# A dilated convolution with shared differences: signs moved into the differences, the first loads in halves, the last outputs on three queues

## The chip, the cores and the metric

The kernel runs on one core of a Trainium2 chip. The metric is device time in microseconds (us), the median of several runs. One further execution is taken with the hardware profiler; its page and its trace are what is read below. Engines are named as on the page: PE is TensorE, PEld its weight load, DVE VectorE, ACT ScalarE, POOL GpSimd, SP SyncE; SPq and ACTq are the DMA issues of SP and ACT.

## The reference

Fifteen taps, two time steps apart, of a causal convolution from 144 to 288 channels, then a gate and a projection:

```python
B, T, D, K = (2, 16000, 144, 15)        # x [B,T,D], w [K,D,2D], w_o [D,D], all bfloat16
xp = jnp.pad(x, ((0, 0), (28, 0), (0, 0)))
h = sum over i of einsum('btc,cd->btd', xp[:, 28 - 2*i : 28 - 2*i + T, :], w[i])
z = jnp.tanh(h[..., :D]) * sigmoid(h[..., D:])
return z @ w_o
```

## The kernel before

**Tiling.** Each of the two sequences is cut into 8 windows of 2000 outputs (16 windows in all), loaded as 2048 + 32 time steps. A window has two octets (`rho` 0 and 1), 32 octets in all; an octet is eight output rows of 128 positions each, 16 time steps apart. The 144 input channels are split into 128 and a remainder of 16.

**Input.** `load` (L82 to L90) brings the 128 channels of a window in by one transposing DMA: the tile `xn`, channels on partitions. The remainder takes two steps. `gather` (L92 to L100) copies the 16 channels, in packets of 32 bytes, from DRAM to a DRAM scratch `xg`, sorted by the time step modulo 4 (`r=4` blocks). `remainder` (L102 to L105) then reads `xg` back by a transposing DMA so that eight taps of 16 channels lie on the 128 partitions: the tile `rx`.

**Sharing by differences.** The convolution of eight output rows isn't done tap by tap. Sums of weights are multiplied with the signal, and other weights with differences of the signal in time, and results are shared between rows, so that an octet takes 72 matmuls of 128x128 by 128x288 where each row by itself would take more. `derive_steps` (L111 to L141) makes the differences on VectorE: d2, d4, d8 from `xn`, d48 from d4, d28 and d24 from d2, and `re` (L129 to L137, two instructions) from `rx`. Where a difference is needed with the other sign, the weights are negated: `a1e`, `an`, `bcn` on VectorE (`neg`, L194), `wn` on ACT (L210), made once at the start from `w_all`, together with the sums `sm`, `ss`, `a1v`, `av`, `bc`, `bcv`, `s_r`, `ns_r` (L197 to L224).

**An octet** has three leaves in the PSUM pool `a` (A1, A2, A3) and two in the pool `bc` (B1, C1). A leaf computes what two rows share (`common`), ACT copies the bank (`copy`), then each row adds its own part (`private`). `direct` (L297) adds the taps on d24 and `re` for the rows B2, B3, C2 and C3, into banks that ACT copied (`dup`). VectorE combines (`q`, `out_y`) in FP32; ACT does tanh and sigmoid; VectorE multiplies to `z`. A transposing DMA on SP turns `z` to `zt` (`z_load`, L330), 12 matmuls project it (`outproj`, L351), ACT copies to the output tile `o` (`project_out`, L359), and `store` (L364) writes a window of 125 rows of 4608 bytes, issued on SP.

**Order.** The order is written by hand: `PLAN` (L16 to L23) lists the steps of one octet with an offset in octets, and `todo` (L441) sorts all octets' steps by octet plus offset, then by place in the list. Each engine and queue works in that order. `xg:-6` places a gather six octets ahead of the octet that uses it, `xl:-3` a load, `rx0:-2` the read of the scratch. `late` (L226) puts `re` and `d24` of the first window where they are first needed. SP's queue thus carries, for each window: a gather, a load, an rx, two zt and a store. Buffers: two of `xn` and `rx`, two of `o`, two PSUM banks for `a`, five for `bc`, one for `po`.

**Start.** The remainder's weights come by 15 small DMAs, seven from POOL (`wo_p`) and eight from ACT (`we_r`), L181 to L184. The first load, `w_all` in four parts (L178, L179) and the first rx are on SP, the first gather on ACT. TensorE does 20 warm-up matmuls on zeros.

**End.** The last octet's `z` is transposed by TensorE (`z_by_pe`, L335). Five stores remain after the last convolution matmul, all on SP: window 14 whole, one half of window 15 (rows of 288 bytes), and the other half in three pieces (L431 to L434).

Of the kernel before, what the change touches and what calls it, by code (L numbers as in the profile page):

```python
# [9 lines left out]
F32 = mybir.dt.float32  # L10
# [6 lines left out]
    po0:3 yB2_0:0 m0a:1 g1:3 q3_0:0 ost:4 pA3_1:0 sg1:1 kC:0 B2_1:0 q3_1:0 po1:3 vA1:-1 g2:3 pC_0:0  # L17
    yB2_1:0 th1:1 kA1:-1 po2:3 B3_0:0 d28:-2 pA1_0:-1 dC_0:0 pA1_1:-1 d48:-1 pC_1:0 xg:-6 xl:-3 C2_0:0
    yB3_0:0 a1s_0:-1 m1a:1 vA2:-1 yB3_1:0 a1s_1:-1 m0b:1 dC_1:0 kA2:-1 yC2_0:0 sg0:0 C3_0:0 zt:2 C3_1:0
    d4:-2 d8:-2 m1b:1 re:-1 th0:0 pA2_0:-1 vB:-1 q2_0:-1 pA2_1:-1 kB:-1 yC3_1:0 C2_1:0 q2_1:-1 vA3:-1  # L20
    yC2_1:0 yC3_0:0 kA3:-1 pB_0:-1 dB_0:-1 pB_1:-1 g0:2 d24:-2 d2:-3 dB_1:-1 vC:-1 pA3_0:-1 B2_0:-1
    B3_1:-1 rx0:-2
# [4 lines left out]
def kernel(  # L27
# [27 lines left out]
    WB = H + WT  # L55
    assert T >= WT and T % 16 == 0
# [35 lines left out]
    def gather(wi, eng=nc.sync):  # L92

        b, t0, _, _ = wins[wi]
        lo = H if t0 == 0 else 0
        dst = xg[wi, 0:WB, :].rearrange("(r j) c -> r j c", r=4)
        if lo:
            nc.gpsimd.dma_start(out=dst[:, 0:lo // 4, :], in_=zero[0:4, 0:lo // 4 * CR].rearrange("r (j c) -> r j c", c=CR))
        eng.dma_start(out=dst[:, lo // 4:, :],  # L99
                      in_=x[b, t0 - H + lo:t0 + WT, CM:D].rearrange("(j r) c -> r j c", r=4))  # L100

    def remainder(wi):  # L102
        rx = xa_pool.tile([P, WB], BF16, name="rx")
        nc.sync.dma_start_transpose(out=rx[:], in_=bass.AP(xg.tensor, xg[wi, 0:1, 0:1].offset, [[CR, WB], [1, P]]))
        sets[wi]["rx"] = rx  # L105

    def runs(t, first, step, n, count, off=0):

        return bass.AP(t.tensor, t[:, first + off:first + off + 1].offset, [t.ap[0], [step, count], [1, n]])

    def derive_steps(s):  # L111
        ahead = {"x": 0}

        def sub(name, of, d, first=0, step=None, n=None):
            ahead[name] = ahead[of] + d
            hi = WB - ahead[name]

            def go(eng=nc.vector):
                t = xd_pool.tile([P, WB], BF16, name=name)
                if step is None:  # L120
                    o, a, b_ = t[:, 0:hi], s[of][:, d:d + hi], s[of][:, 0:hi]
                else:
                    count = (hi - first - n) // step + 1
                    o, a, b_ = (runs(t_, first, step, n, count, off) for t_, off in ((t, 0), (s[of], d), (s[of], 0)))
                eng.tensor_tensor(out=o, in0=a, in1=b_, op=ALU.subtract)  # L125
                s[name] = t
            return go

        def re():  # L129
            t = xd_pool.tile([P, WB], BF16, name="re")  # L130
            o, a = (t_[:].rearrange("p (r j) -> p r j", r=4) for t_ in (t, s["rx"]))
            n = WB // 4 - 7
            for r, d in ((0, 0), (2, 1)):
                nc.vector.tensor_tensor(out=o[:, r:r + 2, 0:n], in0=a[:, 2 - r:4 - r, d:d + n], in1=a[:, r:r + 2, 0:n],
                                        op=ALU.subtract)
            s["re"] = t

        return dict(d4=sub("d4", "x", 4, 0, 4, 2), d2=sub("d2", "x", 2), d8=sub("d8", "x", 8, 0, 8, 2),
                    d48=sub("d48", "d4", 8, 0, 4, 2), d28=sub("d28", "d2", 8, 6, 8, 4),
                    d24=sub("d24", "d2", 4), re=re)  # L140
# [30 lines left out]
    nc.gpsimd.memset(w_all[:, K, :], 0.0)  # L171
    nc.gpsimd.memset(wo_p[0:CR, :], 0.0)
    xg = dram.tile([NW, WB + CR, CR], BF16, name="xg")
    nc.gpsimd.dma_start(out=xg[:, WB:, :].rearrange("w j c -> w (j c)"), in_=zero[0:NW, 0:CR * CR])
    sets = [None] * NW
    sets[0] = load(0)
    gather(0, nc.scalar)
    for c in range(0, 16, 4):  # L178
        nc.sync.dma_start(out=w_all[:, c:min(c + 4, K), :], in_=w[c:min(c + 4, K), 0:CM, :].rearrange("k c d -> c k d"))  # L179
    remainder(0)  # L180
    for t, first, eng in ((wo_p, 1, nc.gpsimd), (we_r, 0, nc.scalar)):  # L181
        for k in range(first, K, 2):
            g = (14 + first - k) // 2
            eng.dma_start(out=t[g * CR:(g + 1) * CR, :], in_=w[k, CM:D, :])  # L184
# [6 lines left out]
    for k in ("d8", "d4", "d48", "d2", "d28"):  # L191
        pre0[k]()

    def neg(o, a):  # L194
        nc.vector.tensor_scalar_mul(o, a, -1.0)
# [4 lines left out]
    a1e = wtile(2, "a1e")  # L200
    av = const.tile([CM, 2, 2, D2], BF16, name="av")
    an = const.tile([CM, 2, 2, D2], BF16, name="an")
    wq = w_all[:].rearrange("p (j i e) d -> p j i e d", i=2, e=2)
    wn = const.tile([CM, 4, 2, D2], BF16, name="wn")
    for c in range(4):
        add(sm[:, 2 * c:2 * c + 2, :], w_all[:, 4 * c:4 * c + 4:2, :], w_all[:, 4 * c + 1:4 * c + 4:2, :])
        add(ss[:, c, :], sm[:, 2 * c, :], sm[:, 2 * c + 1, :])
        if c % 2:
            add(a1v[:, c // 2, :], ss[:, c - 1, :], ss[:, c, :])
        nc.scalar.mul(out=wn[:, c], in_=wq[:, c, 1], mul=-1.0)  # L210
    neg(a1e[:], ss[:, 1:4:2, :])
    quad = sm[:].rearrange("p (j i e) d -> p j i e d", i=2, e=2)
    add(av[:], quad[:, :, 0], quad[:, :, 1])
    neg(an[:], quad[:, :, 1])
    s_r = const.tile([P, D2], BF16)
    add(s_r[:], we_r[:], wo_p[:])
    ns_r = const.tile([P, D2], BF16)
    neg(ns_r[:], s_r[:])
    bc = const.tile([CM, 4, 2, D2], BF16, name="bc")
    add(bc[:], wq[:, :, 0], wq[:, :, 1])  # L220
    bcv = const.tile([CM, 2, 2, D2], BF16, name="bcv")
    add(bcv[:], bc[:, 0:4:2], bc[:, 1:4:2])
    bcn = const.tile([CM, 2, 2, D2], BF16, name="bcn")
    neg(bcn[:], bc[:, 1:4:2])  # L224

    late = [({"dB_0", "dB_1", "dC_0", "dC_1"}, pre0["re"]), ({"dB_0", "dB_1", "dC_0", "dC_1"}, pre0["d24"])]  # L226
    ident = const.tile([P, P], BF16)
    make_identity(nc, ident[:])

# [7 lines left out]
    def st_r(t, off):  # L237
        c0 = (off + 4) % 4 * (WB // 4) + (off + 4) // 4
        return t[:, c0:c0 + 4 * (P - 1) + 1:4]

    class Leaf:


        def __init__(self, s, is_a, sig, dsig, off, v, e, o, rem=None):
            self.s, self.is_a, self.other = s, is_a, {}
            self.a = (sig, dsig, off, v, e, o, rem)

        def common(self):
            sig, dsig, off, v, e, o, rem = self.a
# [12 lines left out]
        def private(self, i):  # L262
            sig, dsig, off, v, e, o, rem = self.a
            f, o_ = ((e, off - 8), (o, off))[i]
            for j in range(2):
                mm(self.ts[i], st(self.s[dsig], o_ - 16 * j), f(j), False, rem is None and j == 1, True)
# [4 lines left out]
    class Octet:  # L271
        def __init__(self, s, rho):
            self.s, self.rho = s, rho
            self.A1 = Leaf(s, True, "x", "d8", rho, lambda j: a1v[:, j, :], lambda j: a1e[:, j, :], lambda j: ss[:, 2 * j, :])
            self.A2 = Leaf(s, True, "d4", "d48", rho - 4, lambda j: av[:, j, 1, :], lambda j: an[:, j, 1, :],
                           lambda j: sm[:, 4 * j + 1, :], ("rx", rho, ns_r[:]))
            self.A3 = Leaf(s, True, "d4", "d48", rho, lambda j: av[:, j, 0, :], lambda j: an[:, j, 0, :],
                           lambda j: sm[:, 4 * j, :], ("rx", rho + 4, s_r[:]))
            self.B1 = Leaf(s, False, "d2", "d28", rho - 2, lambda j: bcv[:, j, 1, :], lambda j: bcn[:, j, 1, :],
                           lambda j: bc[:, 2 * j, 1, :])  # L280
            self.C1 = Leaf(s, False, "d2", "d28", rho, lambda j: bcv[:, j, 0, :], lambda j: bcn[:, j, 0, :],
                           lambda j: bc[:, 2 * j, 0, :])
# [19 lines left out]
        def B2(self, i):  # L302
            self.direct(self.B1.ts[i], self.rho - 6 + 8 * i, lambda j: wn[:, j, 1, :], 3, "re", self.rho - 2 + 8 * i, wo_p[:])
# [4 lines left out]
        def C2(self, i):  # L308
            self.direct(self.C1.ts[i], self.rho - 4 + 8 * i, lambda j: wn[:, j, 0, :], 4, "re", self.rho + 8 * i, we_r[:])
# [25 lines left out]
    def z_by_pe(z):  # L335
        zt = zt_pool.tile([P, 9, P], BF16, name="zt")
        for i, g0 in enumerate(range(0, 9, 4)):
            n = min(4, 9 - g0)
            ps = (bank(True) if i else ps_o.tile([P, 512], F32, name="po", tag="po"))[:].bitcast(BF16).rearrange("p (g m) -> p g m", m=256)
            for k in range(n):  # L340
                nc.tensor.transpose(ps[:, k, 0:P], z[:, g0 + k, :], ident[:])
            copy_by(i, zt[:, g0:g0 + n, :], ps[:, 0:n, 0:P])
        return zt

    def copy_by(i, o, a):
        if i % 2:
# [4 lines left out]
    def outproj(o, g, end):  # L351
# [7 lines left out]
    def project_out(o, ob, rho, g, end):  # L359
        r0, n = 3 * g, min(3, 8 - 3 * g)  # L360
        copy_by(1 - g % 2 if end else 1, ob[:, rho + 2 * r0:rho + 2 * (r0 + n - 1) + 1:2, :],
                o.po[g][:, 0:n * D].rearrange("p (r e) -> p r e", e=D))
# [113 lines left out]
```

## Time and profile before

| | |
|---|---|
| median of 3 runs | 363.47 us (362.69 to 364.66) |
| profiled execution: time, span | 363.42 us, 361.6 us |
| mean granted TensorE clock | 0.961 |
| PE, PEld busy | 328.1 us (91%), 306.6 us (85%) |
| DVE, ACT busy | 291.5 us (81%), 242.7 us (67%) |
| DMA | 144358 packets, 38.25 MB; 140255 packets under 512 bytes |
| queue q1 (SP) | 141406 packets, 77.4% of 16 engines' time |

The page cuts the span into 40 slices of about 9 us; a digit is the busy share in tenths. A busy row for PE counts matmuls that overlap, so it is read together with what TensorE waited for. The DMA share is the mean over 16 DMA engines: a transfer that uses only some of them can't bring it near 1. The landing records of the trace give one mark for each part of a transfer that comes to its end.

### The profile page before, as it was taken

How to read it: one execution, taken by the hardware profiler on the slowest of the kernel's cores; microseconds unless marked ns; L12 is line 12 of the kernel's file. 1: busy time of each engine (PE TensorE's matmuls, PEld its weight loads, DVE VectorE, ACT ScalarE, POOL GpSimd, SP SyncE). 2: the span in 40 equal slices, each digit the busy share in tenths (PEclk: the TensorE clock that was granted, in tenths of full speed). 3: DMA queues.
4: the chain of work that ended last, by engine and by line, in shares of the span. 5: the costliest groups of instructions: out<-in, count | busy, mean ns of one | idle time of the engine just before them, and what ended most of it. 6: DMA issues, size and time to landing. Idle time of an engine off the chain costs nothing.

```text
span 361.6 us, 7336 instructions
## 1 busy us (share of the span) xinstructions
PE 328.1 (91%) x2685; PEld 306.6 (85%) x2685; DVE 291.5 (81%) x664; ACT 242.7 (67%) x581; POOL 11.9 (3%) x30
## 2 busy tenths in 40 slices
PE   7184999999999999999999999999999999999830
PEld 2052999999999999999999999999999999999820
DVE  4564899898988898889888988898898989886620
ACT  1221667777777777777777777877777777777730
POOL 8400000000000000000000000000000000000000
PEclk9776999999999999999999999999999999999985
DMA  8547847787989696797979796979689498323323
GB/s 190 84 11 91 103 94 97 91 87 103 139 96 147 108 131 125 107 129 104 138 55 148 102 151 103 134 114 127 130 105 144 99 110 140 90 41 66 67 77 51
DMA packets 144358, 38.25 MB, mean 106 GB/s; under 512 B 140255, under 2 KB 142431, under 8 KB 144322
## 3 DMA queue, kind: packets, MB, share of 16 engines
q1 hardware_dynamic: 141406, 37.49, 77.4%
q10 hardware_dynamic: 2308, 0.14, 0.5%
q8 instruction: 21, 0.34, 0.4%
q0 software_dynamic: 608, 0.15, 0.2%
q14 instruction: 15, 0.12, 0.1%
HBM read 2.38 MB, written 10.29 MB: 35 GB/s over the span
## 4 chain that ended last, share of the span: by engine, by line
PE 84%; DMA 5%; SPq 2%; POOL 2%; DVE 2%; ACT 1%; issue 1%; DVEq 0%; ACTq 0%; POOLq 0%
PE bc L231 53%; PE a L231 23%; PE po L357 4%; PE po L354 4%; DMA xn<-in_x_dram 3%; SPq L99 2%; DMA xg<-zero 1%; POOL wo_bd L189 1%; DMA wo_bd<-in_w_o_dram 1%; DVE q L294 1%; DVE y L316 1%; ACT sg L321 1%; ACT o L347 0%; ACT th L321 0%; PE bc L354 0%
## 5 line engine op out<-in xcount | busy, mean ns | idle before, releaser
L231 PEld LDWEIGHTS <-d 128*128 128x128 bf16 x1856 | 232.8, 145 | 14.8 <-issue 6.3
L316 DVE TENSOR_TENSOR y<-q,bc 128x288 f32<-128x288 f32 x256 | 112.9, 451 | 26.0 <-PE bc L231 22.1
L231 PE MATMUL bc<-w_all,d 128*128 128x288 bf16 x512 | 82.8, 287 | 0.0
L231 PE MATMUL bc<-wn,d 128*128 128x288 bf16 x448 | 76.1, 287 | 1.2 <-DVE d L125 1.2
L294 DVE TENSOR_TENSOR q<-a1s,a 128x288 f32<-128x288 f32 x128 | 57.4, 451 | 12.7 <-PE a L231 6.6
L256 ACT COPY a<-a 128x288 f32<-128x288 f32 x96 | 36.8, 383 | 41.3 <-PE a L231 38.6
L260 ACT COPY bc<-bc 128x288 f32<-128x288 f32 x128 | 49.0, 408 | 0.9 <-DVE y L316 0.7
L125 DVE TENSOR_TENSOR d<-xn 128x518 bf16<-128x518 bf16 (+2 forms) x48 | 40.3, 867 | 9.9 <-DMA xn<-in_x_dram 9.9
L347 ACT CAST o<-po 128x432 bf16<-128x432 f32 (+1 forms) x90 | 44.2, 492 | 3.7 <-PE po L357 0.5
L256 ACT COPY bc<-bc 128x288 f32<-128x288 f32 x64 | 24.5, 383 | 31.6 <-DVE y L316 23.1
L321 ACT ACTIVATE sg<-y 128x576 bf16<-128x576 f32 x64 | 45.0, 703 | 0.4 <-DVE z L328 0.4
L321 ACT ACTIVATE th<-y 128x576 bf16<-128x576 f32 x64 | 43.7, 683 | 0.0
L125 DVE TENSOR_TENSOR d<-d 128x1034 bf16<-128x1034 bf16 (+2 forms) x48 | 41.9, 873 | 0.1
L328 DVE TENSOR_TENSOR z<-th,sg 128x64 bf16<-128x64 bf16 (+1 forms) x128 | 38.5, 302 | 1.5 <-ACT th L321 1.5
L231 PE MATMUL bc<-wo_p,re 128*128 128x288 bf16 x128 | 36.8, 287 | 0.0
L231 PE MATMUL bc<-we_r,re 128*128 128x288 bf16 x128 | 36.6, 286 | 0.0
L291 ACT COPY a1s<-a 128x288 f32<-128x288 f32 x64 | 22.7, 404 | 12.8 <-PE a L231 12.6
L357 PEld LDWEIGHTS <-zt 128*128 128x128 bf16 x256 | 22.8, 98 | 9.8 <-issue 1.5
L354 PE MATMUL po<-wo_bd,zt 128*128 128x432 bf16 (+1 forms) x90 | 29.3, 326 | 1.2 <-ACT o L347 1.2
L357 PE MATMUL po<-wo_m,zt 128*128 128x144 bf16 x240 | 29.7, 226 | 0.0
L231 PEld LDWEIGHTS <-re 128*128 128x128 bf16 x256 | 28.8, 113 | 0.1
L231 PE MATMUL a<-an,d 128*128 128x288 bf16 x128 | 26.4, 288 | 0.5 <-ACT a L256 0.5
(58 smaller groups left out, 308.6 us busy)
## 6 DMA issues: line engine op xcount, KB each, us to landing
out_dram<-o SPq DMA_DIRECT2D x15, 562.5 KB
xg<-in_x_dram SPq DMA_DIRECT2D x14, 65.0 KB
w_all<-in_w_dram SPq DMA_DIRECT2D x3, 288.0 KB
zt<-z SPq DMA_TRANSPOSE x31
out_dram<-o SPq DMA_DIRECT2D x1, 281.2 KB
xn<-in_x_dram SPq DMA_TRANSPOSE x16
rx<-xg SPq DMA_TRANSPOSE x16
w_all<-in_w_dram SPq DMA_DIRECT2D x1, 216.0 KB
```

The costliest lines, as they stand in the source:

```text
L125: eng.tensor_tensor(out=o, in0=a, in1=b_, op=ALU.subtract)
L231: nc.tensor.matmul(ps[:, 0:D2], lhsT=l, rhs=r, start=start, stop=stop, skip_group_check=on)
L256: nc.scalar.copy(out=self.ts[1][:, 0:D2], in_=self.ts[0][:, 0:D2])
L260: nc.scalar.copy(out=self.other[i][:, 0:D2], in_=self.ts[i][:, 0:D2])
L291: nc.scalar.copy(out=self.get(cp_pool, "a1s", [P, 2, D2], F32)[:, i, :], in_=self.A1.ts[i][:, 0:D2])
L294: nc.vector.tensor_tensor(out=self.get(cp_pool, name, [P, 2, D2], F32)[:, i, :], in0=self.t["a1s"][:, i, :], in1=leaf.ts[i][:, 0:D2], op=op)
L316: nc.vector.tensor_tensor(out=y[:, k + 4 * i, :], in0=self.t[q][:, i, :], in1=ts[i][:, 0:D2], op=op)
L321: nc.scalar.activation(out=t[:], in_=self.t["y"][:, k::2, lo:lo + D], func=func)
L328: nc.vector.tensor_tensor(out=o, in0=th[:, :, lo:lo + n], in1=sg[:, :, lo:lo + n], op=ALU.mult)
L347: nc.scalar.copy(out=o, in_=a)
L354: nc.tensor.matmul(o.po[g][:, 0:n * D], lhsT=o.zt[:, 8, :], rhs=wo_bd[:, r0:r0 + n, :].rearrange("p r e -> p (r e)"), start=True, stop=False)
L357: nc.tensor.matmul(o.po[g][:, i * D:(i + 1) * D], lhsT=o.zt[:, r0 + i, :], rhs=wo_m[:], start=False, stop=i == n - 1)
```

## The change

**Signs.** `sub` now takes a list of patterns, each with a sign, so that d8, d48, d28 and d24 are each made by two instructions, one for either sign, over every second group. The negated weights `a1e`, `an`, `bcn` and `wn` go; `private` and `direct` use the plain sums and `w_all`.

**Remainder.** The 15 small weight DMAs become two (`raw`), and a matrix `swap` brings the taps into their places on TensorE (`summed`), which also forms `s_r`; ACT copies the results out of PSUM. `bcv` is summed on TensorE as well (`raw_sums`, 16 matmuls with an identity).

**Halves.** The scratch is sorted into two halves by the parity of the time step, of two blocks each, and the gather is two DMAs, in every window. In the first window the two reads of the scratch are separate too, and `re` is made by halves. The first gather, its zeros and the weights are on ACT's queue.

**Order and stores.** `PLAN` is a new list: `xg:-2`, `xl:-3`, `rx0:-1`, and the preparing steps of later windows come after those of the octets in hand. A window's store is issued on ACT. The last three octets are written out by hand (`finish_early`, `finish`): window 14 is stored in two parts of 62 and 63 rows, window 15 in three of 41, 42 and 42, on SP, ACT and POOL.

```diff
-    def gather(wi, eng=nc.sync):
+    def gather(wi, halves=(0, 1), eng=nc.sync):
...
-        eng.dma_start(out=dst[:, lo // 4:, :],
-                      in_=x[b, t0 - H + lo:t0 + WT, CM:D].rearrange("(j r) c -> r j c", r=4))
+        for h in halves:
+            dst = xg[wi, h * HB:h * HB + 2 * NJ, :].rearrange("(k j) c -> k j c", k=2)
+            if lo:
+                eng.dma_start(out=dst[:, 0:lo // 4, :], in_=zero[0:2, 0:lo // 4 * CR].rearrange("k (j c) -> k j c", c=CR))
+            eng.dma_start(out=dst[:, lo // 4:, :],
+                          in_=x[b, t0 - H + lo:t0 + WT, CM:D].rearrange("(j k h) c -> h k j c", k=2, h=2)[h])
...
+            def go():
+                t = s[name] = xd_pool.tile([P, WB], BF16, name=name)
+                for first, step, inner, sign in sets_ or ((0, hi, [[1, hi]], 1),):
...
+                    nc.vector.tensor_tensor(out=o, in0=a, in1=b_, op=ALU.subtract)
...
+                    d8=sub("d8", "x", 8, (0, 16, pair, 1), (8, 16, pair, -1)),
+                    d48=sub("d48", "d4", 8, (12, 16, [[4, 2]] + pair, 1), (4, 16, [[4, 2]] + pair, -1)),
+                    d28=sub("d28", "d2", 8, (14, 16, quads, 1), (6, 16, quads, -1)),
+                    d24=sub("d24", "d2", 4, (6, 8, quads, 1), (2, 8, quads, -1)), re=re)
...
+    nc.scalar.dma_start(out=raw[:, 0, :], in_=w[0:K:2, CM:D, :])
+    nc.scalar.dma_start(out=raw[0:P - CR, 1, :], in_=w[1:K:2, CM:D, :])
...
+    gather(0, (0,), nc.scalar)
+    gather(0, (1,), nc.scalar)
...
-    remainder(0)
-    for t, first, eng in ((wo_p, 1, nc.gpsimd), (we_r, 0, nc.scalar)):
-        for k in range(first, K, 2):
-            g = (14 + first - k) // 2
-            eng.dma_start(out=t[g * CR:(g + 1) * CR, :], in_=w[k, CM:D, :])
+    remainder(0, (0,))
+    remainder(0, (1,))
...
+    def summed(parts, outs):
...
+        for i, (l, r) in enumerate(parts):
+            nc.tensor.matmul(t[:, 0:D2], lhsT=l, rhs=r, start=i == 0, stop=i == len(parts) - 1)
+        for o, sign in outs:
+            nc.scalar.mul(out=o, in_=t[:, 0:D2], mul=sign)
...
-        nc.scalar.mul(out=wn[:, c], in_=wq[:, c, 1], mul=-1.0)
-    neg(a1e[:], ss[:, 1:4:2, :])
...
-    def store(wi, o, eng=nc.sync, first=0, last=15, step=1):
+    def store(wi, o, parts):
...
-        eng.dma_start(out=to[:, first:last + 1:step, :], in_=o[m0:m1, first:last + 1:step, :])
+        for i, eng in enumerate(parts):
+            a, e = ((m1 - m0) * k // len(parts) for k in (i, i + 1))
+            eng.dma_start(out=to[a:e], in_=o[m0 + a:m0 + e, :, :])
...
-            store(wi, outs[n])
+            store(wi, outs[wi], [nc.scalar])
...
+        store(NW - 2, outs[NW - 2], [nc.sync, nc.gpsimd])
...
+        store(NW - 1, outs[NW - 1], [nc.sync, nc.scalar, nc.gpsimd])
...
+    todo = sorted((n + at, n > 1 and n + at < 0, i, n, name) for i, (name, at) in enumerate(plan) for n in range(NO)
```

## The prediction

> **What bounds the kernel now.** The page comes first: the slices, and the chain that ended last.
>
> ```profile
> PE   7184999999999999999999999999999999999830
> PEclk9776999999999999999999999999999999999985
> DMA  8547847787989696797979796979689498323323
> ...
> PE 84%; DMA 5%; SPq 2%; POOL 2%; DVE 2%; ACT 1%; issue 1%; DVEq 0%; ACTq 0%; POOLq 0%
> ```
>
> TensorE is full from the sixth slice to the end of the 37th. The start (three slices, part of it at a lower granted clock) and the end (two) are not. Two single octets, and then short stretches in which only one kind of transfer ran, from the busy times by stretch (columns: stretch, length, PE, PEld, DVE, ACT, POOL, granted clock, DMA share, GB/s):
>
> ```profile
> 65.59:75.41 9.82, 9.82 (x85) 9.44 (x84) 8.82 (x21) 7.44 (x18) 0.00 (x0) 1.00 0.68 96
> 242.50:252.32 9.82, 9.82 (x85) 9.43 (x84) 8.82 (x21) 7.44 (x18) 0.00 (x0) 1.00 0.86 116
> ```
> ```profile
> 200.00:201.00 1.00, 1.00 (x12) 0.95 (x10) 0.96 (x3) 1.00 (x3) 0.00 (x0) 1.00 1.26 286
> 205.00:207.00 2.00, 2.00 (x20) 1.87 (x19) 2.00 (x6) 1.07 (x4) 0.00 (x0) 1.00 0.47 11
> 214.00:216.00 2.00, 2.00 (x19) 1.97 (x17) 1.84 (x6) 1.07 (x3) 0.00 (x0) 1.00 0.31 94
> ```
>
> An octet is 9.82 us of TensorE without a gap (32 of them are 314 us), so a window is 19.64 us, and nothing in the change takes matmuls out of it. Gains can come only from start and end. The second fence gives the price of each kind of transfer: a transpose load of 256-byte packets moves 286 GB/s, a gather of 32-byte packets 11 GB/s, a store 94 GB/s. SyncE's queue in one window, from the timeline:
>
> ```profile
> 201.52 0.69 SPq L99 DMA_DIRECT2D xg<-in_x_dram  x1
> 203.63 4.16 SPq L332 DMA_TRANSPOSE zt<-z  x1
> 207.88 1.98 SPq L104 DMA_TRANSPOSE rx<-xg  x1
> 211.09 0.28 SPq L367 DMA_DIRECT2D out_dram<-o  x1
> 211.47 6.73 SPq L89 DMA_TRANSPOSE xn<-in_x_dram  x1
> ```
>
> The zt behind the gather is held 4.16 us, the xn behind the store 6.73 us: the queue is one file, and it is full for some 18 of 19.64 us. It is hidden, but barely.
>
> Start and end, from the waits and the timeline:
>
> ```profile
> DVE d L125 <- DMA xn<-in_x_dram: 9.9, 2, 5.4
> PE a L231 <- DVE q L294: 5.2, 1, 5.2
> ```
> ```profile
> 14.60 5.96 SPq L99 DMA_DIRECT2D xg<-in_x_dram  x2
> 20.60 7.63 SPq L89 DMA_TRANSPOSE xn<-in_x_dram  x1
> ```
> ```profile
> 344.55 12.00 SPq L367 DMA_DIRECT2D out_dram<-o  x5
> ```
>
> The load of window 1 stands behind two gathers and lands at 30.60; VectorE's subtraction d2 waits 5.41 us for it, and TensorE goes on only at 32.65. At the end the last convolution matmul is over at 341.6, and the five stores stretch the span to 361.6: 20.0 us.
>
> **How many engines a transfer uses.** The landing records of the trace come in 16 parts for a transpose over 128 partitions, in 4 for a gather (4 blocks outermost at its source), in 5 for a store of 125 rows. So rows are dealt out in equal shares, and the outermost count sets the number of shares: 125 = 5 x 25. Two gathers issued back to back (14.60) ran one after the other at 11 GB/s, not side by side, so they share the same four engines. At 11 GB/s a gather moves 338 packets a us, 84.5 an engine: 11.8 ns a packet; the 2080 packets are 520 an engine, 6.15 us. The packet starts repeat every 47 ns, four packets of one engine, which looks like an engine's own pace. I take it that every narrow transfer starts from the same engine, as those two did. A store at 94 GB/s is 20.4 rows a us over five engines: 0.25 us a row, 6.25 us for 25 rows; its DMA share of 0.31 is 5/16.
>
> The change makes two gathers of a window's one, each with **two** blocks outermost. By these rows each runs in two shares of 520: the same 2080 packets now on two engines, 1040 each, 12.3 us a window instead of 6.15. The 41 rows of the last store on SyncE have no divisor from 2 to 16, so they go in one share; 62 rows go in 2, 42 in 14.
>
> The Trainium skill's "DMA: Bandwidth & Descriptors", section "Why a DMA increments its semaphore by 16 and not by 1", states this rule (the largest number up to 16 that divides the slowest dimension on both sides) and that SP and ACT use the lowest-numbered engines: with it gathers, stores and the 41 rows all meet on engine 0, and the sum is the forecast below. The same page's rule that a spread over several queues brings no bandwidth would by itself leave the end where it is.
>
> **The change, part by part.**
>
> *Weight work.* VectorE loses a1e 0.40, an 0.45, s_r 0.31, ns_r 0.23, bcv 0.76, bcn 0.45: 2.6 us, and its wait of 3.9 us for we_r. ACT loses four wn (2.7 us) and the eight we_r issues that held it until 15.0; it gains eight copies of 128x288 out of PSUM at 0.38, 3.1 us. TensorE gains 20 matmuls of 128x288, 0.12 to 0.24 us each by the clock, in a stretch where it idles: nothing. The first private matmuls of A1 can start at about 13.6 instead of 17.8.
>
> *Subtractions in two halves.* Four more VectorE instructions a window. Below: one fixed part each, about 0.1 us, 0.2 us an octet. Above: each half costs its whole row (0.67, 0.69, 0.69, and 2 x 0.69 for 1.23), 2.2 us a window, 1.1 an octet, on 8.82 of 9.82: just full. I take 0.3, hidden; the upper end would cost up to 3 us in all.
>
> *First loads.* ACT now waits for xn (landed 5.5) before it issues the first half gather; the copies of s_r and the rest stand behind it, harmless. First half: from 6.2, 512 packets an engine, 6.05 us, and about 2.5 us for sharing with w_all until 9: landed at 15. Second half: 21. SyncE waits for it before the second rx, and behind that wait stands the load of window 1: rx 0.95, xn 1.85, landing about 1.2: 25.0 instead of 30.6. With 13 matmuls more done ahead of that wait than before (56 against 43 in TensorE's order), 1.6 us, the start gains 5.6 + 1.6 = 7.2 us.
>
> *Transfers in the steady part.* The store goes to ACT's queue, the gathers stay on SyncE's. A ring of them from one rx to the next: rx 1.85, zt 1.0, xn 1.85, gather 12.3 and 0.35 to land (the other zt runs in its end), 17.35 us. That is below 19.64. But the store's 25 rows must pass the same two engines. At the start, where the gather on ACT's queue met w_all on SyncE's, the packet records count 30 a us and engine of the one and 31 of the other: queues take turns packet by packet. So 25 rows of 0.25 us let only 25 gather packets through, and the store adds up to 6.25 us: 23.6 us a window, 4 more than TensorE needs. If rows cost only their shortest duration in the trace, 0.18 us, 21.8; if the store hid wholly, 19.64 stays.
>
> The sum: the window-1 gather follows xn at 24.0 and lands at 36.7. One ring without a store, 17.4; thirteen with one (stores of windows 0 to 12 beside gathers 3 to 15), 13 x 23.6 = 306.8: the last rx starts at 360.9, lands at 363.2. From there octets 29 (its last 40%), 30 and 31, 2.4 x 9.82 = 23.6: last convolution matmul at 386.8 (341.6 before).
>
> *End.* The other parts of the end save about 0.5 us (one output copy fewer between the last activations). Engine 0 then gets 31 rows of the 62, all 41, and 4, 3 and 3 of the other queues: 82 rows, at 0.18 to 0.25 us 14.6 to 20.5 us, from 3.3 us after the last matmul, and 2.2 us to the end as before (359.4 to 361.6): 20.1 to 26 us, against 20.0. Three queues save nothing if the shares are so.
>
> Upper end: 386.8 + 26 = 412.8; lower, with rows of 0.18 us: 363.4 + 20.1 = 383.5. The profiled run has 1.8 us outside its span (363.42 against 361.6), and is as good as the median of 363.47. So 385 to 415. The busy share of 5/16 speaks for the long rows, packets of two queues in flight at once for the short: I take **405 us**.
>
> **Rivals.**
> 1. *The store hides beside the gather* (two packets of an engine are in flight in a gather: its share of 0.47 is 7.5 engines' worth on four). Then 19.64 stays: 341.6 - 7.2 = 334.4, with the end 20.1 to 26 and 1.8: 356 to 362, say 359. It decides where the store adds under 2.2 us a window, or where its five engines are not the gather's.
> 2. *The other side: the gather's rate is not an engine's.* If 338 packets a us is what memory takes, two shares are as fast as four. The halves then land at 11 and 14.5, window 1 at 18.5, before VectorE comes to it (about 21): y at 23 instead of 31.8, 8.8 + 1.6 + 1 for the clock: 11.4 us. 330.2 and an end of 20.1 to 26: 352 to 358; with even shares in the last store too, an end of 12: 344. Say 353. Against it: the 47 ns beat. It decides with the rate of one gather in the steady part.
> 3. *The new order stalls TensorE by itself* (VectorE full, a buffer late): 365 to 370.
>
> **Chances.** Forecast 0.60, rival 1 0.15, rival 2 0.20, rival 3 0.05. Only the forecast's own range is 385 to 415; the range over all, 350 to 416, leaves out the lower part of rival 2 and the far end. About 0.5% is what can be told from no change. Faster by more: rival 2 and two thirds of rival 1, 0.30; within: 0.05; slower: 0.65.
>
> **What would show it.** Right: stretches with a 32-byte gather alone at 5 to 6 GB/s, SyncE's zt behind it held 10 us, VectorE waiting for rx or xn in each window, TensorE gaps of about 4 us a window from the fourth on; a last store trickling at 18 to 26 GB/s. Wrong: 11 GB/s as before; an octet of 9.82 us throughout; the span ending 12 us after the last matmul. The start is right if window 1 lands near 25.

## The result, and the profile after

The changed kernel takes **427.09 us** (median of 4 runs, 424.76 to 431.99) against 363.72 us before (4 runs): ratio 1.172, 95% interval 1.163 to 1.181. The forecast, 405 us, had the direction and not enough of the size; its range ended at 416. Ratios, here and in the table, leave out a run more than 1.5% above the fastest of its kernel (here 431.99 us). The profiled execution took 424.76 us, its span is 423.0 us.

The page of the changed kernel: the slices, then the chain of work that ended last, by engine and by line:

```profile
PE   7489979699976969997696999689699957999940
PEclk9659989999996988999698999979799996999995
DMA  8543473958828294982829487574929728492240
...
PE 55%; DMA 37%; ACTq 2%; SPq 1%; issue 1%; ACT 0%; POOLq 0%
PE bc L248 32%; DMA zt<-z 30%; PE a L248 16%; DMA xg<-in_x_dram 5%; PE po L370 4%; PE po L373 3%; ACTq L101 2%; DMA w_all<-in_w_dram 1%; DMA rx<-xg 1%; SPq L91 1%; SPq L109 0%; SPq L102 0%; ACT th L336 0%; PE bc L370 0%; POOLq L516 0%
```

TensorE, full from the sixth slice on before, now has a hole (a stretch without work) in every second or third slice. With each of the nine holes of 3.1 to 6.6 us between 55 and 352 us its granted clock falls to a half, for 3.4 or 6.8 us. DMA holds 37% of the chain that ended last, 30% the transposition `zt<-z` alone; DMA held 5% before. SyncE's queue over one window (start, length of the issue, line, transfer):

```profile
257.69 5.35 SPq L102 DMA_DIRECT2D xg<-in_x_dram  x2
263.15 11.91 SPq L347 DMA_TRANSPOSE zt<-z  x1
276.27 2.04 SPq L109 DMA_TRANSPOSE rx<-xg  x1
278.42 1.31 SPq L347 DMA_TRANSPOSE zt<-z  x1
279.83 1.85 SPq L91 DMA_TRANSPOSE xn<-in_x_dram  x1
```

The zt behind the two gathers is held 11.91 us; in the kernel before it was 4.16. The rx issues of windows 5 and 14 lie 9 x 24.5 us apart (over all from window 2 to window 15 it is 24.0 a window); TensorE needs 19.64. And who waits (engine, line, for what: total us, times, longest):

```profile
PE po L370 <- DMA zt<-z: 43.3, 10, 6.6
...
DVE d L126 <- DMA xn<-in_x_dram: 4.4, 1, 4.4
```

TensorE waits for zt in the projection; VectorE waits for a load once, at the start. Busy times by stretch in the same window and the next (stretch, length, PE, PEld, DVE, ACT, POOL, granted clock, DMA share, GB/s):

```profile
270.00:272.00 2.00, 0.86 (x8) 0.57 (x5) 1.54 (x4) 1.28 (x3) 0.00 (x0) 1.00 0.25 97
272.00:274.00 2.00, 0.00 (x0) 0.00 (x0) 0.00 (x0) 0.00 (x0) 0.00 (x0) 1.00 1.83 109
276.00:278.00 2.00, 1.20 (x7) 0.83 (x8) 0.00 (x0) 0.26 (x1) 0.00 (x0) 0.50 0.32 61
278.00:280.00 2.00, 2.00 (x10) 1.40 (x9) 1.27 (x3) 1.19 (x3) 0.00 (x0) 0.50 1.22 270
286.00:288.00 2.00, 2.00 (x19) 1.97 (x18) 1.84 (x4) 1.41 (x4) 0.00 (x0) 1.00 0.24 5
```

Three things stand here. First, a gather alone moves 5 GB/s (last line; 11 before). Second, TensorE stands still for six us, and then (third and fourth lines) runs at half its clock: 10 matmuls in 2 us, not 19. Third, the landing records tell why the store makes it worse. These are the times of the parts of one store (125 rows, five parts) and of the half gather beside it (two parts); one early mark, soon after the issue of each, is left out:

```
store   271.55  271.80  272.00  275.27  275.45
gather  276.13  276.14
```

Three parts of the store are done by 272.0, the two others 3.4 us later. From 266 to 269, when the store began, the half gather still made 129 to 190 packets a us; from 269 to 274 it made 43 in all. Between 272 and 274 the packet records count 22 gather packets and 21 rows: where only the two late parts were left, one packet of the one let one of the other through.

The end: the last convolution matmul is over at 402.4, the span at 423.0. In the last stretch only the 41 rows on SyncE still run:

```profile
416.00:421.00 5.00, 0.00 (x0) 0.00 (x0) 0.00 (x0) 0.00 (x0) 0.00 (x0) 0.50 0.06 27
```

A DMA share of 0.06 is one engine of 16, at 27 GB/s.

### The profile page after: what moved, and what is told of

Read it like the earlier page. It is cut to its first block, busy times and chain, and to the rows that moved or that the text cites. A ratio compares the mean times of both kernels' runs of the same rounds, so it can differ in the third digit from the quotient of the medians.

```text
span 423.0 us, 7527 instructions
## 1 busy us (share of the span) xinstructions
PE 351.4 (83%) x2705; PEld 315.4 (75%) x2705; DVE 304.8 (72%) x726; ACT 242.5 (57%) x583; POOL 8.7 (2%) x24
## 4 chain that ended last, share of the span: by engine, by line
PE 55%; DMA 37%; ACTq 2%; SPq 1%; issue 1%; ACT 0%; POOLq 0%
PE bc L248 32%; DMA zt<-z 30%; PE a L248 16%; DMA xg<-in_x_dram 5%; PE po L370 4%; PE po L373 3%; ACTq L101 2%; DMA w_all<-in_w_dram 1%; DMA rx<-xg 1%; SPq L91 1%; SPq L109 0%; SPq L102 0%; ACT th L336 0%; PE bc L370 0%; POOLq L516 0%
## 5 line engine op out<-in xcount | busy, mean ns | idle before, releaser
L248 PEld LDWEIGHTS <-d 128*128 128x128 bf16 x1856 | 236.5, 146 | 14.4 <-issue 2.1
L248 PE MATMUL bc<-w_all,d 128*128 128x288 bf16 x960 | 161.7, 292 | 1.3 <-DVE d L126 1.0
L331 DVE TENSOR_TENSOR y<-q,bc 128x288 f32<-128x288 f32 x256 | 114.3, 451 | 22.4 <-PE bc L248 19.6
L309 DVE TENSOR_TENSOR q<-a1s,a 128x288 f32<-128x288 f32 x128 | 53.6, 452 | 73.9 <-PE a L248 72.6
L370 PE MATMUL po<-wo_bd,zt 128*128 128x432 bf16 (+1 forms) x88 | 31.2, 355 | 43.3 <-DMA zt<-z 43.3
L278 ACT COPY bc<-bc 128x288 f32<-128x288 f32 x128 | 50.5, 395 | 23.7 <-PE bc L248 22.6
L126 DVE TENSOR_TENSOR d<-d 128x516 bf16<-128x516 bf16 (+1 forms) x96 | 59.6, 667 | 0.0
L248 PE MATMUL a<-sm,d 128*128 128x288 bf16 x256 | 55.8, 311 | 0.6 <-ACT a L274 0.5
L248 PE MATMUL bc<-bc,d 128*128 128x288 bf16 x256 | 50.7, 302 | 0.0
L370 PEld LDWEIGHTS <-zt 128*128 128x128 bf16 x96 | 9.7, 101 | 48.6 <-DMA zt<-z 47.2
L126 DVE TENSOR_TENSOR d<-xn 128x260 bf16<-128x260 bf16 (+2 forms) x64 | 42.6, 690 | 4.4 <-DMA xn<-in_x_dram 4.4
L343 DVE TENSOR_TENSOR z<-th,sg 128x512 bf16<-128x512 bf16 (+1 forms) x128 | 35.6, 302 | 0.0
L373 PEld LDWEIGHTS <-zt 128*128 128x128 bf16 x256 | 24.4, 104 | 10.0 <-issue 2.5
```

Of the source, the lines that this page charges most:

```text
L126: nc.vector.tensor_tensor(out=o, in0=a, in1=b_, op=ALU.subtract)
L248: nc.tensor.matmul(ps[:, 0:D2], lhsT=l, rhs=r, start=start, stop=stop, skip_group_check=on)
L278: nc.scalar.copy(out=self.other[i][:, 0:D2], in_=self.ts[i][:, 0:D2])
L309: nc.vector.tensor_tensor(out=self.get(cp_pool, name, [P, 2, D2], F32)[:, i, :], in0=self.t["a1s"][:, i, :], in1=leaf.ts[i][:, 0:D2], op=op)
L331: nc.vector.tensor_tensor(out=y[:, k + 4 * i, :], in0=self.t[q][:, i, :], in1=ts[i][:, 0:D2], op=op)
L343: nc.vector.tensor_tensor(out=o, in0=th[:, :, lo:lo + n], in1=sg[:, :, lo:lo + n], op=ALU.mult)
```

## The experiments

The theory under test is that of the prediction, *shares*: a gather's time is its packets on one DMA engine, and two blocks outermost leave it two engines. The rivals are *memory* (the rate of small packets has nothing to do with engines) and *order* (the new list, zt or the store badly placed, or VectorE full). The shares of a transfer were read from the landing records.

| kernel | median us | ratio to before, 95% | us a window, rx 5 to rx 14 | last convolution matmul |
|---|---|---|---|---|
| changed | 427.09 | 1.163 to 1.181 | 24.5 | 402.4 |
| wide | 352.22 | 0.968 to 0.973 | 19.6 | 329.7 |
| before_two_halves | 432.64 | 1.188 to 1.196 | 23.3 | 408.9 |
| no_store | 373.86 | 1.025 to 1.033 | 20.3 | 349.7 |
| store_wide | 387.65 | 1.063 to 1.069 | 21.0 | 365.2 |
| gather_on_act | 471.43 | 1.295 to 1.300 | 27.3 | 448.8 |
| gather_on_pool | 530.65 | 1.448 to 1.462 | 32.2 | 507.4 |
| halves_apart_sync | 397.83 | 1.089 to 1.098 | 22.4 | 373.5 |
| halves_apart_act | 375.83 | 1.031 to 1.041 | 20.5 | 351.9 |
| even_end | 419.63 | 1.148 to 1.158 | 23.6 | 404.0 |
| before_wide_even | 343.67 | 0.943 to 0.947 | 19.7 | 330.8 |
| both | 342.43 | 0.940 to 0.943 | 19.6 | 330.0 |
| both_one_queue | 342.37 | 0.939 to 0.943 | 19.6 | 330.3 |

### The number of shares

**wide.** The changed kernel; only the order of the loops inside each gather is turned over.

```diff
-            eng.dma_start(out=dst[:, lo // 4:, :],
-                          in_=x[b, t0 - H + lo:t0 + WT, CM:D].rearrange("(j k h) c -> h k j c", k=2, h=2)[h])
+            eng.dma_start(out=dst[:, lo // 4:, :].rearrange("k j c -> j k c"),
+                          in_=x[b, t0 - H + lo:t0 + WT, CM:D].rearrange("(j k h) c -> h j k c", k=2, h=2)[h])
```

> The changed kernel, with the time step j outermost in each half gather instead of the block k: the same packets to the same places, dealt out in 13 shares (520 = 13 x 40; 16 in the first window of a sequence) instead of 2. Theory of shares (a gather's time is its packets on one engine): a half takes 80 packets x 11.8 ns = 1 us instead of 6.1, the zt behind it is held under 3 us instead of 11, TensorE has no gap after the start, a window takes 19.64 us, and with the end as it is (20.7 us) the time is 350 to 358 us. Theory of memory (the 32-byte packets set 338 a us, whatever the engines): at most back to four shares' 6.15 us, 356 to 365. Theory of order (gather, store or zt badly placed in the new list, or VectorE too full): 400 to 427, as the changed kernel.

352.22 us, 75 less than the changed kernel, from one loop order. A half gather now lands in 13 parts, and the 2080 packets of a window go out between 228.06 and 229.74 us. Page and SyncE's queue of this kernel:

```profile
PE   8679999999999999999999999999999999999810
...
PEclk9899999999999999999999999999999999999975
```
```profile
223.08 1.31 SPq L347 DMA_TRANSPOSE zt<-z  x1
224.48 1.96 SPq L91 DMA_TRANSPOSE xn<-in_x_dram  x1
226.49 1.70 SPq L102 DMA_DIRECT2D xg<-in_x_dram  x2
232.82 1.32 SPq L347 DMA_TRANSPOSE zt<-z  x1
```

The zt is held by nothing, and between the start and the end TensorE has no hole and no lowered clock. Memory falls, and so does the rival that the new order stalls by itself: VectorE is busier (301.9 us against 291.5 before), and that is hidden. The end is as long as in the changed kernel (20.6 us). The new loop order also changes the order of the addresses, which this run doesn't separate from the number of parts; the next one keeps the order inside each block.

**before_two_halves.** The kernel before, with only its gather cut in two.

```diff
-        eng.dma_start(out=dst[:, lo // 4:, :],
-                      in_=x[b, t0 - H + lo:t0 + WT, CM:D].rearrange("(j r) c -> r j c", r=4))
+        src = x[b, t0 - H + lo:t0 + WT, CM:D].rearrange("(j r) c -> r j c", r=4)
+        for r in (0, 2):
+            eng.dma_start(out=dst[r:r + 2, lo // 4:, :], in_=src[r:r + 2])
```

> The kernel before, with each gather cut into two DMAs of two blocks, nothing else. Theory of shares: 2080 packets on two engines instead of four, 6.15 us more on a queue that is full for 18 of 19.64 us: 24.2 us a window, the time 415 to 435 us. Theory of order or of the other parts of the change: only one issue more, 363 to 367 us.

432.64 us: this edit alone costs the kernel before as much as the whole change did. Each half lands in two parts, at 169 packets a us (340 for the whole gather before). Its SyncE queue is one full file, from xn to xn 24.6 us:

```profile
218.20 7.82 SPq L89 DMA_TRANSPOSE xn<-in_x_dram  x1
226.11 1.31 SPq L333 DMA_TRANSPOSE zt<-z  x1
227.47 5.42 SPq L101 DMA_DIRECT2D xg<-in_x_dram  x2
233.00 6.83 SPq L333 DMA_TRANSPOSE zt<-z  x1
239.92 2.28 SPq L105 DMA_TRANSPOSE rx<-xg  x1
242.30 0.43 SPq L368 DMA_DIRECT2D out_dram<-o  x1
242.84 7.36 SPq L89 DMA_TRANSPOSE xn<-in_x_dram  x1
```

### The store beside the gather

**no_store** leaves out the stores of windows 0 to 13 (`store(...)` becomes `pass`), **store_wide** cuts each store at row 80, into 16 and 15 shares instead of 5:

```diff
...
-            store(wi, outs[wi], [nc.scalar])
+            store(wi, outs[wi], [nc.scalar] * 2, (80, 45))
```

> The changed kernel without the stores of windows 0 to 13: their part of the output is left out. Theory of shares with the store taking turns: the ring of a window falls from 24.3 to about 17.4 us, below TensorE's 19.64, the gaps go, and the time is 352 to 360 us. Theory that the gather alone is enough, because the zt behind it on SyncE's queue is held 10 us and TensorE has no work in hand for so long: gaps stay in most windows, 385 to 420.

> The changed kernel with each window's store cut into 80 and 45 rows (16 and 15 shares instead of 5), both on ACT's queue; the gathers stay on two shares. If the store costs because its 25 rows stand on the gather's two engines: 8 rows are left there, so 17 x 0.2 to 0.25 us go, 3.4 to 4.2 of the 4.2 us a window between the changed kernel and the one without stores: 375 to 385 us. If it costs as bytes or by its place in the list: 420 to 430 us.

373.86 us, between the two theories, and 387.65, a little over the 375 to 385 of the shares. TensorE's wait for zt in the two, first no_store, then store_wide:

```profile
PE po L370 <- DMA zt<-z: 9.1, 6, 2.5
```
```profile
PE po L370 <- DMA zt<-z: 18.7, 12, 3.5
```

43.3 us of waiting become 9.1 without stores, and 18.7 with all the bytes stored but on more engines. So most of the cost lies in where the rows stand, not in their bytes. Without any store some stalls are left: of the 20 us by which the last convolution matmul comes later than in wide, 12 are lost by 58 us, at the start (269 TensorE instructions done against 372, at 9.82 us for 85), and the rest in the windows, 20.3 us each and not TensorE's 19.64. From 50 us on the waits of no_store are 2.5 us at most, and its clock is full until the last stores. In store_wide, from 50 us on, three waits are longer than 3 us, and they are the ones that a half clock follows.

### The place in the queue

**gather_on_act** issues the gathers on ACT's queue (`gather(wi, (0, 1), nc.scalar)`).

> The changed kernel with all gathers issued on ACT's queue, where the stores are, instead of SyncE's; the shares stay two. Theory of the engine (what counts is the sum on the lowest engine: gather 12.3, store 6.25, xn 1.85, rx 1.85, two zt 2.0 = 24.2 us a window, by whatever queue): 24.2 us a window stays, 415 to 430 us. Theory of the file (zt stands behind the gather on SyncE's queue, and is only held there): zt is held 1 to 2 us, TensorE is full, 352 to 362 us.

471.43 us: slower than either theory said. ACT's own instructions, and TensorE's longest wait in this kernel:

```profile
238.53 5.66 ACTq L102 DMA_DIRECT2D xg<-in_x_dram  x2
244.23 0.68 ACT L336 ACTIVATE sg<-y 128x576 bf16<-128x576 f32 x1 [5.33 <-issue]
```
```profile
PE bc L248 <- ACT bc L274: 74.6, 15, 5.8
```

The issue of the second half behind the first takes 4.95 us, and ACT stands for 5.3 us (in wide both issues together took 1.70 us, on SyncE). SyncE has nothing to compute; ACT has PSUM to copy, and TensorE waits for that. The run didn't separate the theories, so two more put the halves an octet apart: **halves_apart_sync**, shown here, and **halves_apart_act**, with `nc.scalar` in both places.

```diff
-    pA3_1:0 xg:-2 sg0:1 ...
+    pA3_1:0 xg:-3 xh:-2 sg0:1 ...
...
-            gather(wi)
+            gather(wi, (0,), nc.sync)
             return
+        if name == "xh":
+            gather(wi, (1,), nc.sync)
+            return
...
```

> The changed kernel with the two half gathers an octet apart on SyncE (the first at three octets ahead, the second at two) instead of back to back; two shares each. Theory of the file (TensorE stands still because a zt is held behind two gathers, 12 us, more than its slack of some 6): each zt is held 6 us at most, fits its slack but for the store, and the time falls to 360 to 385 us. Theory of the engine (24 us of work a window on the two lowest engines): 410 to 430 us.

> The same halves, an octet apart, on ACT's queue, so that no second gather is issued while the first fills the queue, and no zt stands behind a gather in a file. Theory of the file: TensorE full, 352 to 362 us. Theory of the engine: the two engines still have 24 us of work a window, and zt, rx and xn wait for them: 410 to 430 us.

397.83 and 375.83 us: both lie between the two theories, and neither forecast was met. On ACT's queue, SyncE's queue and TensorE's waits look like this:

```profile
219.82 4.40 SPq L109 DMA_TRANSPOSE rx<-xg  x1
224.31 1.31 SPq L347 DMA_TRANSPOSE zt<-z  x1
225.71 4.94 SPq L91 DMA_TRANSPOSE xn<-in_x_dram  x1
231.81 1.31 SPq L347 DMA_TRANSPOSE zt<-z  x1
```
```profile
PE bc L248 <- ACT bc L274: 9.9, 10, 4.9
PE a L248 <- DMA rx<-xg: 3.9, 4, 3.0
```

The same packets on two shares, the same store, and a window of 20.5 us: so the work on the lowest engines, 24.2 us a window by the sum of the expectation, is no bound. Above wide it stays 23.6 us, 12.5 of them lost by 58 us (264 instructions done against 372). On SyncE's queue, apart, the zt still stood up to 7.7 us behind a half gather, and a window took 22.4 us; there TensorE waited more for rx (14.3 us after 58 us) than for zt (6.2). With two shares, then, the price is set mostly by what is queued behind the gather.

**gather_on_pool** issues them on POOL's queue (`gather(wi, (0, 1), nc.gpsimd)`).

> The changed kernel with the gathers on POOL's queue, where an issue that is held up holds nothing else; two shares as before. Theory of the engine (24 us a window of work on the two lowest engines by whatever queue): 24 us a window, 415 to 430 us. Theory of the file (what costs is the zt held behind the gather on SyncE, and the second issue that holds its engine): TensorE full, 352 to 365 us.

530.65 us, a miss for both. A half gather took 15.0 us from issue to landing there (the median), against 8.4 on SyncE's (257.7 to 266.1 in the changed kernel). And it was another transfer: the records of POOL's queue show some 115 packets of 256 bytes for a half, not 1040 of 32, up to 15 of them at once, and from 222 to 226 us each took some 750 ns. So the run changed the transfer along with the queue, to a slower one, and it tells nothing of the file.

### The end, and a version that beats both

**even_end**: the changed kernel; the last stores are cut where the rows divide.

```diff
...
-        store(NW - 2, outs[NW - 2], [nc.sync, nc.gpsimd])
+        store(NW - 2, outs[NW - 2], [nc.sync, nc.gpsimd], (80, 45))
...
-        store(NW - 1, outs[NW - 1], [nc.sync, nc.scalar, nc.gpsimd])
+        store(NW - 1, outs[NW - 1], [nc.sync, nc.scalar, nc.gpsimd], (48, 45, 32))
```

> The changed kernel with the last stores cut into parts that deal out evenly: window 14 in 80 and 45 rows (16 and 15 shares) instead of 62 and 63, window 15 in 48, 45 and 32 (16, 15, 16) instead of 41, 42 and 42; the same three queues. Theory of shares: the lowest engine has 5+3+3+3+2 = 16 rows instead of some 80, the span ends 5 to 7 us after the last matmul instead of 15.2, and the time is 8 to 10 us under the changed kernel's, 415 to 420 us. Theory that the bytes or the late issues set the end: no change, 424 to 430 us.

419.63 us (416.64 to 421.60). From the last matmul to the end it is 5.5 us, 15.2 in the changed kernel. On SyncE's queue the 80 and the 48 rows land in 16 parts, on ACT's the 45 in 15; on POOL's every transfer leaves 16 marks, the 63 rows of the changed kernel too, so that its shares can't be read there. The median fell by 7.5, less than those 9.7, in a kernel whose runs differ by 5 to 7 us. One more run of it, whose label names another kernel, gave 423.42:

> A second look at the same kernel as even_end, for the spread between executions: within 4 us of it.

**both** joins the edits of wide and even_end; **both_one_queue** issues its five last stores on SyncE alone.

> The changed kernel with j outermost in the gathers (13 or 16 shares) and the evenly dealt last stores together. Theory of shares: 352.2 less 8 to 10 us of the end, 341 to 345 us. If the end is set otherwise: 350 to 353 us.

> As both, with all five last stores issued on SyncE instead of three queues. If queues bring no bandwidth of their own and only the shares count: within 1 us of both. If the three queues bring the gain: 3 us or more above it.

342.43 and 342.37 us, 5.9% under the kernel before: three queues bring nothing over one, and the even shares bring the whole gain of the end. Page of both, and the stretch in which the last stores run:

```profile
PE   8679999999999999999999999999999999999982
...
PEclk9799999999999999999999999999999999999998
```
```profile
336.50:339.00 2.50, 0.00 (x0) 0.00 (x0) 0.00 (x0) 0.00 (x0) 0.34 (x1) 0.96 0.79 229
```

229 GB/s where the changed kernel had 27.

**before_wide_even**: the kernel before, with the two edits and nothing else of the change.

```diff
-        eng.dma_start(out=dst[:, lo // 4:, :],
-                      in_=x[b, t0 - H + lo:t0 + WT, CM:D].rearrange("(j r) c -> r j c", r=4))
+        eng.dma_start(out=dst[:, lo // 4:, :].rearrange("r j c -> j r c"),
+                      in_=x[b, t0 - H + lo:t0 + WT, CM:D].rearrange("(j r) c -> j r c", r=4))
...
+        for a, e in ((0, 80), (80, 125)) if wi >= NW - 2 else ((0, 125),):
...
```

> The kernel before, with the time step outermost in its gather (13 or 16 shares instead of 4) and the last two windows' stores cut at row 80 (16 and 15 shares instead of 5); nothing else of the change. By shares: window 1's load no longer waits 6 us for gathers at the start, and the end is 5 to 8 us shorter: 349 to 355 us. What this kernel lacks against both is what the signs, the sums on TensorE, the halves and the new list are worth: 7 to 12 us if they were worth what the start of the wide run suggests; about 0 if the gain was all in the gather.

343.67 us, below the 349 to 355 expected, and within 1.3 us of both, with overlapping intervals. 10.8 us come from the start (last convolution matmul at 330.8, before 341.6), 8.6 from the end (11.4 us, before 20.0). What the signs, the sums on TensorE, the halves and the new list are worth beside that is about 1 us, and not clear of the intervals.

## Why the prediction was right in its direction and wrong in its size

**Right.** The two shares and their pace came out: 5 GB/s alone, 171 packets a us where 169 were worked out. The "Why a DMA increments its semaphore by 16 and not by 1" section of the Trainium skill's "DMA: Bandwidth & Descriptors" gives the number of shares as the largest number up to 16 that divides the slowest dimension on both sides. On the queues of SyncE and ACT the landing records agree for every count seen (2, 13, 15, 16, and one for 41 rows). The zt was to be held 10 us and was held 11.91. The store took turns with the gather, packet for packet. The end took 20.6 us, in the 20.1 to 26 that was given, with 5.8 rows a us in its last stretch, 0.17 us a row. The added subtractions are hidden, as was said: VectorE's 10.4 us more in wide, with 2.6 us of weight work gone, are 13 over 32 octets, 0.41 an octet where 0.3 was taken. One reading was off: SyncE's issues before took 16.0 of 19.64 us (mean of ten windows), not some 18.

**The step that failed: the ring.** "A ring of them from one rx to the next ... 17.35 us. That is below 19.64" and then "23.6 us a window". The sum took the queue's transfers for the only bound, and so had VectorE wait for rx and xn. That zt would be held 10 us it gave as a sign, but no term priced TensorE's wait for it. Three runs say otherwise. Without stores a window took 20.3 us, not 19.64; with them 24.5; and with the same packets on the same shares, but no zt behind them, 20.5. What ties the loop is one held transposition: gather, zt held behind it, projection on TensorE, and the next z later for it, so that TensorE's work and the transfer add up in the chain instead of running side by side (the chain: PE 55%, `zt<-z` 30%). That 23.6 came near the 24.5 was luck: the ring without a store was put at 17.35 and measured 20.3, and the store was put at 6.25 and measured 4.2.

**What the wait costs beyond itself** had no term. Against wide the span is 72.7 us longer. Of these, 11.9 are lost by 58 us (103 instructions). After that 40.2 us are waits for zt (43.3 less the 3.1 that ended at 58.4). TensorE's busy time from there is 307.5 us, against 275.4 in wide and 11.9 for the instructions that are left: 20.2 more. That goes with the granted clock, at half for 51.2 us between 58 and 403. The sum is 72.3. By the section "HAM oscillation — how this bites in real kernels" of the Trainium skill's "TensorE: Matmul & The Clock Gate", which prices time at half clock at half of it, 51.2 us would cost an estimated 25.6. Measured were 20.2; in 13.4 us of that time TensorE stood idle. The clock was not varied by itself in any run; its share is read from the busy times only.

**The start**: a gain of 7.2 us was forecast. At 50 us the changed kernel had run 228 TensorE instructions against 186, 20 of them the new sums: 22 x 0.116 = 2.5 us. By 58 us nothing of it is left (269 against 249, the 20 sums again): TensorE had its first wait for zt, 3.1 us. The gathers landed as worked out (15.9 and 21.9; 15 and 21), window 1 at 27.2 instead of 25.0. But "the copies of s_r and the rest stand behind it, harmless" was wrong: the issue of a small DMA behind the first gather held ACT for 6.78 us, the copies waited until 14.05, and TensorE 2.8 us for one of them; the first private matmuls of A1 came at 16.7, not 13.6.

**Rivals.** Rival 2, that the rate is not an engine's, is refuted by the 5 GB/s and by wide; rival 1, that the store hides, by no_store; rival 3 by wide.

**Where the sum lost its time.** The last convolution matmul ended at 402.4, not 386.8. Of these 15.6 us, 2.7 came before the rx of window 1 was issued (39.4, not 36.7), 1.2 in the first ring, 5.3 in the thirteen others, and 6.3 behind the issue of the last rx (370.2, not 360.9; its issue was held until 376.4, and 26.0 instead of 23.6 us follow).

**Open.** The records don't name the engines, so that store and gather meet on the lowest is inferred from the two late parts. Why a gather on POOL's queue takes 15 us stays open, and so does why a held issue takes as long as it does.

## What to carry to other kernels

Before a DMA is cut in two, count the outermost dimension of both halves: the cut can halve the engines it runs on, and then nothing is gained; turning the loops so that a long, divisible dimension is outermost was worth 75 us here, and row counts that divide evenly in the last stores another 10 (352.2 to 342.4). The change's other parts, with both of these in place, were worth about 1 us over the kernel before, not clear of the intervals. When a transfer gets slower, look at what is queued behind it and who waits for that, before adding up bytes; and price a recurring TensorE stall of several us with the slow clock that follows it, here half as much again; the waits of up to 2.5 us in no_store cost no clock.

## What was not expected of the hardware

- An issue can hold its engine: behind a half gather on two shares the next DMA, of 512 bytes, took 6.78 us to issue on ACT at the start (0.51 in wide); a second half gather took 4.7 us in the steady part on SyncE, 4.95 on ACT.
- A gather starts faster than it goes on: on four shares 542 and 572 packets in the first two us, then 340 a us; on two shares 249 and 285 in the first two us, then some 170 a us. On 13 shares all 2080 went in 1.7 us, over 1200 a us.
- The changed kernel is less steady than wide: 424.8 to 432.0 us in four runs, against 351.8 to 353.5. Not every held-up kernel is: gather_on_act, the slower of the two, took 470.3 to 472.3.
